# Tiles 4 to 7 transposed by VectorE, one spreading product for four tiles' scales, and VectorE for gate times up in the head

## The chip, the cores and the metric

The kernel runs on one core of a Trainium2 chip. The metric is device time in microseconds. The kernel before takes 787.4 us, the median of 3 runs (787.26 to 787.54). A core has TensorE (matrix products into PSUM), VectorE, ScalarE and GpSimd (element-wise work), SyncE (SP, which issues the DMAs here) and DMA engines. Each engine takes its own instructions strictly in the order in which the program lists them, and waits for others by semaphores.

## The reference

```python
def _A_ref(x, wqkv, wo):              # S = 2048, D = 640, 32 heads of 20
    qkv = (x @ wqkv) ...              # q, k, v
    idx = pos[:, None] - arange(8) * 2      # 8 earlier positions, two apart
    logits = einsum(q, kg) * scale          # kg, vg: k and v at idx
    attn = softmax(where(idx >= 0, logits, -1e9))
    return (attn weighted sum of vg) @ wo

def _B_ref(x, w_gate, w_up, w_down):  # F = 1536
    return ((x @ w_gate) * (x @ w_up)) @ w_down

xn = layernorm(x)
out = x + _A_ref(xn, wqkv, wo) * silu(_B_ref(xn, w_gate, w_up, w_down))
```

## The kernel before

**Tiles.** The 2048 rows are 16 tiles of 128. Tiles 0 to 7 hold the even positions, 8 to 15 the odd ones, as attention looks at positions two apart. The normalised rows are wanted transposed, as operands of TensorE: `xT` has four chunks of four tiles, each in a high and a low part (`hi`, `lo`). Every product is three products of such parts (`mm3`, L90 to L95: hi by hi, hi by lo, lo by hi).

**Two ways to transpose.** Tiles 0 to 7 go through `trans` (L218): VectorE scales the tile (`norm`, `apply`), TensorE transposes it in five pieces into PSUM, ScalarE copies out the high part and VectorE subtracts to get the low part. Tiles 8 to 15 go through `trans_odd` (L245): the tile is loaded a second time in another layout (`load_xq`, from `xq`), in which 32 x 32 blocks lie so that VectorE's own transpose (L249) makes the tile that is wanted. In that layout a partition holds pieces of four different rows, so mean and scale have to be spread to other partitions: `spread` (L236) does it by four products with the selection matrix `sel` for all eight tiles. The tile then takes four scalings of 160 columns, a transpose, a copy of the high part on ScalarE, and a subtraction for the low part, which `halves` holds back until the next tile has been transposed (`low_parts`).

**Units and pieces.** The heads are in six groups (5, 5, 5, 5, 6, 6); a unit is one group for the even or the odd positions, 12 in all. `qkv(u, i)` (L281) is q, k and v of unit u for tile i: 15 matmuls into one of four PSUM buffers "q", which ScalarE empties by two copies, into `kv` (L289) and `q` (L290). There are two `kv` buffers, one for even and one for odd units, so unit 2 writes where unit 0's attention reads. `attention(u)` (L298) is VectorE's, but for the exponentials on ScalarE (L333): four products and sums for the logits (L321, L324), the softmax, then four weighted products (L342) with sums between (L350) and the output (L353). `gate_up(f, ch)` (L379) is a piece: 15 matmuls for g, 15 for u, of 128 columns of F and 512 rows, each into one of two PSUM buffers. ScalarE copies g to `gs` (L389); the product of gate and up comes in `finish`: on VectorE (L400) while an attention is running, else by a copy of u on ScalarE (L402) and a product on GpSimd (L403). The result goes to DRAM. `finish` is called in the middle of the next piece, or at once where no attention is running.

**Order.** The order is written by hand: an engine's order is the order of the calls. Attention is a generator. `advance(budget)` adds to a credit, and lays down attention's next steps as long as the credit is above zero; each step takes its cost from it (1.85 for one of the large steps with 5 heads, 1.5 for a group of three small ones). A piece gives 3.25 in its middle and 3.25 at its end, a `qkv` 1.9. `begin_unit(u)` follows a `drain(u - 2)`, which lays down all that is left of that unit's attention.

**The head** (L656 to L702) normalises tiles 4 to 7 together, lays their TensorE transposes between pieces (0, 0) and (1, 0), then goes on with pieces (0, 1) and (1, 1) and the odd tiles. The first attention starts in unit 1 at i = 3; pieces (0, 2), (1, 2), (0, 3), (1, 3) follow, and from L733 on the units and pieces alternate.

Of the kernel before, what the change touches and what calls it, by code (L numbers as in the profile page):

```python
# [50 lines left out]
def kernel(  # L51
# [23 lines left out]
    def st(shape, tag, bufs, dt=F32):  # L75
        cnt[0] += 1
        return sb.tile(shape, dt, tag=tag, bufs=bufs, name=f"{tag}_{cnt[0]}")

    def pt(shape, tag, bufs):
        cnt[0] += 1  # L80
        return ps.tile(shape, F32, tag=tag, bufs=bufs, name=f"{tag}_{cnt[0]}")
# [37 lines left out]
    def load_wf(f):  # L119
        wf_raw[f] = st([P, KD, 2, P], "wraw", 3)  # L120
        nc.sync.dma_start(wf_raw[f], wgu[f])
# [58 lines left out]
    def moments(s0, n, mv=None):  # L180
        stats = st([P, n, 2, 6], "stats", 2)
        mv = st([P, n, 2], "mv", 2) if mv is None else mv
        for i in range(n):
            for a in range(2):
                nc.vector.bn_stats(stats[:, i, a, :], xt[s0 + i][:, a * HALF:(a + 1) * HALF])
            nc.vector.bn_aggr(mv[:, i, :], stats[:, i])
        return mv

    def rstd(var, out, n):
        r = st([P, 4, NE], "rstd", 2)[:, :, :n]  # L190
        nc.scalar.activation(r[:, 0, :], var, AF.Sqrt, bias=eps_t)
        step = 1 if n <= 2 else n
        for i in range(0, n, step):
            nc.vector.tensor_scalar_add(r[:, 1, i:i + step], var[:, i:i + step], EPS)
        nc.vector.reciprocal(r[:, 2, :], r[:, 0, :])
        if step == 1:
            for i in range(n):
                ve, a, b = (r[:, k, i:i + 1] for k in (1, 2, 3))
                nc.vector.tensor_scalar(b, a, a, ve, op0=ALU.mult, op1=ALU.mult)
                nc.vector.tensor_scalar(b, b, -0.5, 1.5, op0=ALU.mult, op1=ALU.add)  # L200
                nc.vector.tensor_scalar(out[:, i:i + 1], b, a, None, op0=ALU.mult)
            return
        nc.vector.tensor_mul(r[:, 3, :], r[:, 2, :], r[:, 2, :])
        nc.vector.tensor_mul(r[:, 3, :], r[:, 3, :], r[:, 1, :])
        nc.vector.tensor_scalar(r[:, 3, :], r[:, 3, :], -0.5, 1.5, op0=ALU.mult, op1=ALU.add)
        nc.vector.tensor_mul(out, r[:, 3, :], r[:, 2, :])

    def apply(y, m, r):
        nc.vector.tensor_scalar(y, y, m, r, op0=ALU.subtract, op1=ALU.mult)

    def norm(s0, n, mv=None):
        mv = moments(s0, n) if mv is None else mv
        r = st([P, n], "r", 2)
        rstd(mv[:, :, 1], r, n)
        for i in range(n):
            apply(xt[s0 + i], mv[:, i, 0:1], r[:, i:i + 1])

    def trans(s):  # L218
        hi, lo = xT_tile(s)
        for k0, k1 in ((0, 4), (4, KD)):  # L220
            p = pt([P, k1 - k0, P], "q", 4)
            for k in range(k0, k1):
                nc.tensor.transpose(p[:, k - k0, :], xt[s][:, k * P:(k + 1) * P], ident)  # L223
            nc.scalar.activation(hi[:, k0:k1, :], p, AF.Copy)  # L224
            nc.vector.tensor_sub(lo[:, k0:k1, :], p, hi[:, k0:k1, :].bitcast(F32))  # L225

    mvo = st([P, NE, 2], "mvo", 1)
    mro = st([P, 2, NE], "mro", 1)  # L230
    mrq = st([P, NQ, 2, NE], "mrq", 1)

    def load_xq(s, n, t):
        nc.sync.dma_start(t, xq[:, s - NE:s - NE + n, :])

    def spread():  # L236

        p = pt([P, NQ, 2, NE], "q", 4)
        for a in range(NQ):
            nc.tensor.matmul(p[:, a], sel[:, a], mro, start=True, stop=True)  # L240
        nc.scalar.activation(mrq, p, AF.Copy)

    halves = []

    def trans_odd(s):  # L245
        for a in range(NQ):
            apply(xt[s][:, a * QC:(a + 1) * QC], mrq[:, a, 0, s - NE:s - NE + 1], mrq[:, a, 1, s - NE:s - NE + 1])
        y = st([P, KD, P], "ot", 2)
        nc.vector.transpose(y.rearrange("p k (q i) -> p k q i", i=QB),  # L249
                            xt[s].rearrange("p (q k j) -> p k q j", q=NQ, j=QB))  # L250
        hi, lo = xT_tile(s)
        nc.scalar.activation(hi, y, AF.Copy)
        low_parts()
        halves.append(lambda: nc.vector.tensor_sub(lo, y, hi.bitcast(F32)))

    def low_parts():
        while halves:
            halves.pop(0)()
# [22 lines left out]
    def qkv(u, i, parts=ALL3):  # L281
        g, r = UN[u]
        c = GROUPS[g] * DH
        p = pt([P, 3 * c], "q", 4)
        hi, lo = xT[(r * NE + i) // TPC]
        t0 = (i % TPC) * P
        a, b = (hi[:, :, t0:t0 + P], lo[:, :, t0:t0 + P]), wq[g]
        mm3(p, [([t[:, k, :] for t in a], [t[:, k, :] for t in b]) for k in range(KD)], parts)
        nc.scalar.activation(kv_t[u][:, :, W - 1 + i, :], p[:, c:].rearrange("p (a c) -> p a c", a=2), AF.Copy)  # L289
        nc.scalar.activation(q_t[u][:, i, :], p[:, :c], AF.Copy)  # L290
        for i0, i1 in ((1, 5), (5, NE)):
            if i == i1 - 1:
                for p0, p1 in ((0, 112), (112, 127)):
                    nc.sync.dma_start(kv_t[u][p0 + 1:p1 + 1, :, i0 - 1:i1 - 1, :],
                                      kv_t[u][p0:p1, :, W - 1 + i0:W - 1 + i1, :])
# [80 lines left out]
    def gate_up_half(f, ch, n, p, c=slice(0, CH), **parts):  # L376
        mm3(p[:, c], [([t[:, k, n, :] for t in wf[f]], [t[:, k, c] for t in xT[ch]]) for k in range(KD)], **parts)

    def gate_up(f, ch, between=(), amid=(), part=None):  # L379
        if part is None:  # L380
            pp = [pt([P, CH], "g", 2), pt([P, CH], "u", 2)]
            c = slice(0, CH)
        else:
            pp, c = part, slice(CH // 2, CH)
        gate_up_half(f, ch, 0, pp[0], c)
        for act in amid:
            act()
        gs = st([P, CH], "gs", 2)
        nc.scalar.activation(gs, pp[0], AF.Copy)  # L389
        for act in between:  # L390
            act()
        share = (c.stop - c.start) / CH
        finish_piece()
        advance(PACE * 3.25 * share)
        gate_up_half(f, ch, 1, pp[1], c)

        def finish():
            hs = st([P, CH], "hs", 2)
            if running:
                nc.vector.tensor_mul(hs, pp[1], gs)  # L400
            else:
                nc.scalar.activation(hs, pp[1], AF.Copy)  # L402
                nc.gpsimd.tensor_mul(hs, hs, gs)  # L403
            nc.sync.dma_start(h_scr[ch * TPC:(ch + 1) * TPC, :, f, :].rearrange("t p c -> p t c"),
                              hs.rearrange("p (t c) -> p t c", c=P))

        unfinished.append(finish)
        if not running:
            finish_piece()
        advance(PACE * 3.25 * share)  # L410

# [2 lines left out]
    def finish_piece():  # L414

        while unfinished:
            unfinished.pop(0)()
# [232 lines left out]
    nc.gpsimd.memset(mask, 0.0)  # L650
    for i in range(NE - 1):
        nc.gpsimd.memset(mask[:, i, :W - 1 - i], MASKED)
    sel = st([P, NQ, P], "sel", 1)
    nc.gpsimd.tensor_copy(sel.rearrange("p q (b i) -> p q b i", i=QB),
                          ident.rearrange("p (q i) -> p q i", i=QB).unsqueeze(2).to_broadcast([P, NQ, NQ, QB]))
    norm(4, 4)  # L656
    qkv(0, 2)
    qkv(0, 3)
    gate_up(0, 0, part=part0)
    trans(4)  # L660
    trans(5)
    moments(8, 2, mvo[:, 0:2])
    gate_up(1, 0, amid=(lambda: trans(6),))
    moments(10, 2, mvo[:, 2:4])
    load_xq(8, 4, xc[:, 4:8])
    trans(7)
    load_wf(2)
    qkv(0, 4)
    qkv(0, 5)
    moments(12, 2, mvo[:, 4:6])  # L670
    moments(14, 2, mvo[:, 6:8])
    load_xq(12, 3, xa)
    load_xq(15, 1, xd)
    nc.vector.tensor_copy(mro[:, 0, :], mvo[:, :, 0])
    rstd(mvo[:, :, 1], mro[:, 1, :], NE)
    gate_up(0, 1, amid=(spread,))
    trans_odd(8)
    trans_odd(9)
    qkv(0, 6)
    trans_odd(10)  # L680
    qkv(0, 7)
    trans_odd(11)
    gate_up(1, 1, amid=(lambda: trans_odd(12),))
    trans_odd(13)
    begin_unit(1)
    for i in range(8):
        if i == 3:
            running.append((0, attention(0)))
        if i == 2:
            load_wq(1, ((0, 3), (3, 5)))  # L690
            low_parts()
        if i < 2:
            trans_odd(14 + i)
        qkv(1, i)
        advance(PACE * 1.9)
    running.append((1, attention(1)))
    split_wq(1, nc.gpsimd)
    gate_up(0, 2)
    gate_up(1, 2)
    gate_up(0, 3)  # L700
    split_wf(2, nc.gpsimd)
# [156 lines left out]
```

## Time and profile before

| | |
|---|---|
| median of 3 runs | 787.4 us |
| the profiled execution | 787.72 us |
| its span, first to last instruction | 785.8 us |
| TensorE busy | 778.8 us |
| VectorE busy | 659.0 us |
| ScalarE busy | 234.7 us |
| GpSimd busy | 147.3 us |
| granted TensorE clock | 1.00 |
| unit 1 on TensorE | from 60.13 us |
| first attention on VectorE | from 69.67 us |
| unit 2 on TensorE | from 104.61 us |
| last attention's output | at 533.46 us |
| output projection on TensorE | from 563.03 us |

In lines of the trace the first two numbers are the start in us from the span's start and the duration of the merged instructions; then come the engine (PE is TensorE, DVE VectorE, ACT ScalarE, POOL GpSimd), the line of the kernel, the operation, what it writes and reads, the shape and the number of instructions, and in brackets the idle time before it and what ended that. Busy times of TensorE overlap at their ends, so its pace is read from start to start. In lists of waits the numbers are us in total, how often, and the longest.

### The profile page before, as it was taken

The page shows a single profiled execution, that of the slowest core. Times are in us where ns is not written, and L with a number is a line of the kernel's source. Part 1 is how long each engine was busy: PE and PEld are TensorE (multiplying, and loading weights), DVE is VectorE, ACT ScalarE, POOL GpSimd, SP SyncE. Part 2 cuts the span into 40 slices and gives each one's busy share as a digit, 9 for nine tenths or more (in the row PEclk, how much of TensorE's full clock was granted, in tenths as well). Part 3 has the DMA queues.
Part 4 walks back from the last instruction along what each step waited for, and adds up shares of the span by engine and source line. Part 5 has one row for each costly group of instructions (what it writes and reads, how often), then busy time and mean ns, then how long its engine had stood idle before and what let it go on. Part 6 is the DMA issues. An engine that isn't in the chain of part 4 may idle for free.

```text
span 785.8 us, 11227 instructions
## 1 busy us (share of the span) xinstructions
PE 778.8 (99%) x4456; PEld 709.7 (90%) x4456; DVE 659.0 (84%) x660; ACT 234.7 (30%) x536; POOL 147.3 (19%) x110
## 2 busy tenths in 40 slices
PE   8999999999999999999999999999999999999997
PEld 6989898889898898899898989888899999999997
DVE  6889899999999979997999999992177667787775
ACT  5334211121112111311221202012366564444442
POOL 5201211022013200410231000112468600000000
PEclk9999999999999999999999999999999999999999
DMA  8272122141132322404033132332797574555534
GB/s 308 80 230 76 41 63 69 48 123 48 50 85 87 96 71 61 118 27 112 28 105 86 58 86 58 102 107 66 164 269 212 165 274 138 195 205 189 181 101 135
DMA packets 81661, 92.68 MB, mean 118 GB/s; under 512 B 23032, under 2 KB 63304, under 8 KB 81480
## 3 DMA queue, kind: packets, MB, share of 16 engines
q1 hardware_dynamic: 81608, 91.96, 38.2%
q8 instruction: 35, 0.57, 0.3%
q14 instruction: 18, 0.15, 0.1%
HBM read 54.53 MB, written 28.31 MB: 105 GB/s over the span
## 4 chain that ended last, share of the span: by engine, by line
PE 99%; DVE 0%; ACT 0%; issue 0%; POOL 0%; POOLq 0%
PE q L95 36%; PE u L95 21%; PE g L95 21%; PE q L598 11%; PE u L598 5%; PE g L598 3%; PE q L157 1%; PE q L223 1%; ACT xc L224 0%; PE q L240 0%; DVE xc L225 0%; DVE q L584 0%; DVE q L585 0%; ACT q L579 0%; POOL ident masks.py:199 0%
## 5 line engine op out<-in xcount | busy, mean ns | idle before, releaser
L95 PE MATMUL u<-xc,wf 128*128 128x512 f32 (+1 forms) x735 | 176.2, 391 | 0.0
L95 PE MATMUL g<-xc,wf 128*128 128x512 f32 (+1 forms) x735 | 176.1, 390 | 0.0
L95 PEld LDWEIGHTS u<-xc,wf 128*128 128x128 f32 x735 | 135.8, 188 | 32.1
L95 PEld LDWEIGHTS g<-xc,wf 128*128 128x128 f32 x735 | 135.4, 188 | 30.9
L95 PE MATMUL q<-wqh,xc 128*128 128x300 f32 (+1 forms) x960 | 159.7, 309 | 1.4 <-DVE xc L225 0.8
L95 PEld LDWEIGHTS q<-wqh,xc 128*128 128x128 f32 x960 | 146.0, 188 | 3.9 <-ACT xc L224 1.4
L321 DVE TENSOR_TENSOR t<-q,kv 128x1600 f32<-128x1600 f32 (+1 forms) x48 | 97.7, 2036 | 10.0 <-DMA kv<-kv 10.0
L342 DVE TENSOR_TENSOR t<-e,kv 128x1600 f32<-128x1600 f32 (+1 forms) x48 | 97.5, 2051 | 1.1
L86 POOL TENSOR_TENSOR wf<-wraw,wf 128x256 fp32r<-128x256 f32 (+2 forms) x22 | 48.5, 2223 | 248.0 <-ACT wf L85 229.8
L324 DVE TENSOR_REDUCE lg<-t 128x80 f32<-128x1600 f32 (+1 forms) x48 | 92.6, 1930 | 1.2
L389 ACT ACTIVATE gs<-g 128x512 f32<-128x512 f32 x48 | 28.7, 598 | 205.9 <-PE g L95 190.8
L95 PE MATMUL q<-wql,xc 128*128 128x300 f32 (+1 forms) x480 | 86.0, 309 | 0.0
L350 DVE TENSOR_TENSOR t<-t,t 128x1600 f32<-128x1600 f32 (+1 forms) x36 | 80.3, 2231 | 1.1
L95 PEld LDWEIGHTS q<-wql,xc 128*128 128x128 f32 x480 | 74.3, 188 | 0.0
L289 ACT ACTIVATE kv<-q 128x200 f32<-128x200 f32 (+1 forms) x96 | 33.4, 348 | 133.0 <-PE q L95 133.0
L598 PE MATMUL q<-xc,wf 128*128 128x320 f32 x432 | 67.3, 309 | 0.0
L598 PEld LDWEIGHTS q<-xc,wf 128*128 128x128 f32 x432 | 64.3, 188 | 0.0
L86 POOL TENSOR_TENSOR wql<-wraw,wqh 128x300 fp32r<-128x300 f32 (+4 forms) x15 | 33.2, 2238 | 142.8 <-ACT wqh L85 137.6
L95 PE MATMUL q<-wf,wf 128*128 128x320 f32 x156 | 35.7, 310 | 0.0
L400 DVE TENSOR_TENSOR hs<-u,gs 128x512 f32<-128x512 f32 x39 | 26.7, 683 | 0.7 <-issue 0.7
L95 PEld LDWEIGHTS q<-wf,wf 128*128 128x128 f32 x156 | 26.1, 189 | 0.0
L86 DVE TENSOR_TENSOR wf<-ot,wf 128x640 fp32r<-128x640 f32 x13 | 14.8, 1137 | 12.8 <-ACT wf L85 12.8
(161 smaller groups left out, 892.2 us busy)
## 6 DMA issues: line engine op xcount, KB each, us to landing
h_scr<-hs SPq DMA_DIRECT2D x48, 256.0 KB, 2.3
wraw<-in_wgu SPq DMA_DIRECT2D x12, 640.0 KB, 5.1
t<-h_scr SPq DMA_DIRECT2D x8, 768.0 KB, 7.2
hs<-s_scr SPq DMA_DIRECT2D x16, 320.0 KB, 4.3
gs<-in_x SPq DMA_DIRECT2D x16, 320.0 KB, 4.7
wraw<-h_scr SPq DMA_DIRECT2D x12, 384.0 KB, 6.0
out<-q SPq DMA_DIRECT2D x14, 320.0 KB, 3.4
wraw<-in_wd SPq DMA_DIRECT2D x12, 320.0 KB, 4.9
```

The costliest lines, as they stand in the source:

```text
L86: eng.tensor_sub(lo, raw, hi.bitcast(F32))
L95: nc.tensor.matmul(acc, a, b, start=first and n == 0, stop=last and n == len(runs) - 1)
L157: nc.tensor.matmul(pt([P, 3, P], "q", 4), ident, ident.unsqueeze(1).to_broadcast([P, 3, P]), start=True, stop=True)
L223: nc.tensor.transpose(p[:, k - k0, :], xt[s][:, k * P:(k + 1) * P], ident)
L289: nc.scalar.activation(kv_t[u][:, :, W - 1 + i, :], p[:, c:].rearrange("p (a c) -> p a c", a=2), AF.Copy)
L321: nc.vector.tensor_mul(t, q.rearrange("p i c -> p (i c)").unsqueeze(1).to_broadcast([P, 2, NE * c]), places(0, j))
L324: nc.vector.tensor_reduce(out=lg[:, :, j:j + 2].rearrange("p n a -> p a n"), in_=heads(t), op=ALU.add, axis=AX.X)
L342: nc.vector.tensor_mul(heads(t), pw, heads(places(1, j)))
L350: nc.vector.tensor_add(acc, acc, t)
L389: nc.scalar.activation(gs, pp[0], AF.Copy)
L400: nc.vector.tensor_mul(hs, pp[1], gs)
L598: nc.tensor.matmul(p, y[:, i, k], wd_t[name][k][:, l], start=new and r == 0, stop=r == len(runs) - 1, skip_group_check=True)
```

## The change

- Tiles 4 to 7 are transposed as the odd tiles are: loaded a second time from `xq`, which now holds tiles 4 to 15, scaled in four parts and transposed by VectorE. `trans_odd` becomes `trans_q`. The twenty TensorE transposes of these tiles go.
- Scales are spread for four tiles at a time, three times in all. `quarter` and a new `sel` replace the four selection matrices: VectorE multiplies the scales by a mask (`own`), and one product with `sel` of 32 columns spreads them.
- In the pieces of the head, and where no attention is running near the end, VectorE multiplies gate by up; only the very last piece keeps ScalarE and GpSimd. Pieces are then finished where `finish_piece` stands in the order, or in the next piece.
- The order of the head is another: pieces, statistics and reloads lie differently, `gate_up(0, 2)` stands between `qkv(1, 3)` and `qkv(1, 4)`, and the first attention starts after it with a credit of -4.

```diff
+    def scales(s0):
+        mv, mr = stat[s0]
+        nc.vector.tensor_copy(mr[:, 0, :], mv[:, :, 0])
+        rstd(mv[:, :, 1], mr[:, 1, :], TPC)
+        own[s0] = st([P, NQ, 2, TPC], "own", 2)
+        nc.vector.tensor_mul(own[s0], mr.unsqueeze(1).to_broadcast([P, NQ, 2, TPC]),
+                             quarter.unsqueeze(2).unsqueeze(3).to_broadcast([P, NQ, 2, TPC]))
+
+    def spread(s0):
+
+        p = pt([P, NQ, 2, TPC], "q", 4)
+        nc.tensor.matmul(p, sel, own[s0], start=True, stop=True)
+        spread_t[s0] = st([P, NQ, 2, TPC], "mrq", 2)
+        nc.scalar.activation(spread_t[s0], p, AF.Copy)
...
-        for a in range(NQ):
-            nc.tensor.matmul(p[:, a], sel[:, a], mro, start=True, stop=True)
-        nc.scalar.activation(mrq, p, AF.Copy)
...
-            if running:
+            if not last:
                 nc.vector.tensor_mul(hs, pp[1], gs)
             else:
                 nc.scalar.activation(hs, pp[1], AF.Copy)
                 nc.gpsimd.tensor_mul(hs, hs, gs)
...
-        if not running:
+        if last:
             finish_piece()
...
-    norm(4, 4)
+    for i in range(TPC):
+        moments_q(4 + i, 1)
+        load_xq(4 + i, 1, xc[:, i:i + 1])
+    scales(4)
+    moments_q(8, 2)
     qkv(0, 2)
     qkv(0, 3)
     gate_up(0, 0, part=part0)
-    trans(4)
-    trans(5)
-    moments(8, 2, mvo[:, 0:2])
-    gate_up(1, 0, amid=(lambda: trans(6),))
-    moments(10, 2, mvo[:, 2:4])
-    load_xq(8, 4, xc[:, 4:8])
-    trans(7)
+    spread(4)
+    trans_q(4)
+    finish_piece()
+    trans_q(5)
+    gate_up(1, 0)
     load_wf(2)
+    trans_q(6)
+    trans_q(7)
     qkv(0, 4)
     qkv(0, 5)
-    moments(12, 2, mvo[:, 4:6])
-    moments(14, 2, mvo[:, 6:8])
+    low_parts()
+    finish_piece()
+    moments_q(10, 2)
+    load_xq(8, 4, xc[:, 4:8])
+    scales(8)
+    qkv(0, 6)
+    qkv(0, 7)
+    moments_q(12, 4)
     load_xq(12, 3, xa)
     load_xq(15, 1, xd)
-    nc.vector.tensor_copy(mro[:, 0, :], mvo[:, :, 0])
-    rstd(mvo[:, :, 1], mro[:, 1, :], NE)
-    gate_up(0, 1, amid=(spread,))
-    trans_odd(8)
-    trans_odd(9)
-    qkv(0, 6)
-    trans_odd(10)
-    qkv(0, 7)
-    trans_odd(11)
-    gate_up(1, 1, amid=(lambda: trans_odd(12),))
-    trans_odd(13)
+    scales(12)
+    gate_up(0, 1, amid=(lambda: spread(8),))
+    trans_q(8)
+    trans_q(9)
+    finish_piece()
+    trans_q(10)
+    gate_up(1, 1, amid=(lambda: spread(12),))
+    trans_q(11)
     begin_unit(1)
-    for i in range(8):
-        if i == 3:
-            running.append((0, attention(0)))
-        if i == 2:
+    trans_q(12)
+    finish_piece()
+    for i in range(TPC):
+        if i == 1:
             load_wq(1, ((0, 3), (3, 5)))
-            low_parts()
-        if i < 2:
-            trans_odd(14 + i)
+        qkv(1, i)
+    trans_q(13)
+    trans_q(14)
+    gate_up(0, 2)
+    trans_q(15)
+    low_parts()
+    credit[0] = -4.0
+    running.append((0, attention(0)))
+    for i in range(TPC, NE):
         qkv(1, i)
         advance(PACE * 1.9)
     running.append((1, attention(1)))
     split_wq(1, nc.gpsimd)
-    gate_up(0, 2)
     gate_up(1, 2)
     gate_up(0, 3)
```

More of the change, by code (lines that the diff above doesn't have):

```diff
@@ L225, in trans, with moments_q, trans_q @@
             nc.vector.tensor_sub(lo[:, k0:k1, :], p, hi[:, k0:k1, :].bitcast(F32))
-    mvo = st([P, NE, 2], "mvo", 1)
-    mro = st([P, 2, NE], "mro", 1)
-    mrq = st([P, NQ, 2, NE], "mrq", 1)
-    def load_xq(s, n, t):
-        nc.sync.dma_start(t, xq[:, s - NE:s - NE + n, :])
-    def spread():
-        p = pt([P, NQ, 2, NE], "q", 4)
-        for a in range(NQ):
-            nc.tensor.matmul(p[:, a], sel[:, a], mro, start=True, stop=True)
-        nc.scalar.activation(mrq, p, AF.Copy)
-    halves = []
-    def trans_odd(s):
-        for a in range(NQ):
-            apply(xt[s][:, a * QC:(a + 1) * QC], mrq[:, a, 0, s - NE:s - NE + 1], mrq[:, a, 1, s - NE:s - NE + 1])
+    stat = {s: (st([P, TPC, 2], "mvo", 3), st([P, 2, TPC], "mro", 3)) for s in range(TPC, NT, TPC)}
+    own, spread_t = {}, {}
+    def moments_q(s, n):
+        s0 = s // TPC * TPC
+        moments(s, n, stat[s0][0][:, s - s0:s - s0 + n])
+    def load_xq(s, n, t):
+        nc.sync.dma_start(t, xq[:, s - TPC:s - TPC + n, :])
+    def scales(s0):
[10 more added lines that the diff above has]
+        nc.scalar.activation(spread_t[s0], p, AF.Copy)
+    halves = []
+    def trans_q(s):
+        m, i = spread_t[s // TPC * TPC], s % TPC
+        for a in range(NQ):
+            apply(xt[s][:, a * QC:(a + 1) * QC], m[:, a, 0, i:i + 1], m[:, a, 1, i:i + 1])
         y = st([P, KD, P], "ot", 2)
@@ L384, in gate_up @@
             pp, c = part, slice(CH // 2, CH)
+        last = (f, ch) == (KF - 1, NCH - 1)
         gate_up_half(f, ch, 0, pp[0], c)
@@ L652 @@
         nc.gpsimd.memset(mask[:, i, :W - 1 - i], MASKED)
-    sel = st([P, NQ, P], "sel", 1)
-    nc.gpsimd.tensor_copy(sel.rearrange("p q (b i) -> p q b i", i=QB),
-                          ident.rearrange("p (q i) -> p q i", i=QB).unsqueeze(2).to_broadcast([P, NQ, NQ, QB]))
-    norm(4, 4)
+    quarter, sel = st([P, NQ], "quarter", 1), st([P, P], "sel", 1)
+    nc.gpsimd.memset(quarter, 0.0)
+    for a in range(NQ):
+        nc.gpsimd.memset(quarter[a * QB:(a + 1) * QB, a:a + 1], 1.0)
+    nc.gpsimd.tensor_add(sel[:, :QB], ident[:, :QB], ident[:, QB:2 * QB])
+    for a in range(2, NQ):
+        nc.gpsimd.tensor_add(sel[:, :QB], sel[:, :QB], ident[:, a * QB:(a + 1) * QB])
+    nc.gpsimd.tensor_copy(sel[:, QB:].rearrange("p (b i) -> p b i", i=QB),
+                          sel[:, :QB].unsqueeze(1).to_broadcast([P, NQ - 1, QB]))
+    for i in range(TPC):
[3 more added lines that the diff above has]
+    moments_q(8, 2)
     qkv(0, 2)
@@ L836 @@
     arrays["xb"] = lay(arrays["x"].reshape(S, NQ, KD, QB).transpose(0, 2, 1, 3).reshape(S, D))
-    odd = arrays["x"].reshape(NQ, QB, NE, DIL, NQ, QC)[:, :, :, 1]
-    arrays["xq"] = lay(odd.transpose(3, 1, 2, 0, 4).reshape(P, NE, D))
+    quarters = arrays["x"].reshape(NQ, QB, NE, DIL, NQ, QC).transpose(3, 4, 1, 2, 0, 5).reshape(DIL, P, NE, D)
+    arrays["xq"] = lay(np.concatenate([quarters[0][:, TPC:], quarters[1]], axis=1))
     q3 = np.asarray(A_wqkv).reshape(D, 3, D)
```

## The prediction

> **What bounds the kernel now.** I read the page first: shares, slices, chain. Then the list of what TensorE waits for, then the order of time of TensorE, ScalarE and VectorE around the instructions that the change touches, and last the distance between each piece's product on VectorE and the matmul that needs its PSUM buffer back.
>
> ```profile
> PE 778.8 (99%) x4456; PEld 709.7 (90%) x4456; DVE 659.0 (84%) x660; ACT 234.7 (30%) x536; POOL 147.3 (19%) x110
> PE 99%; DVE 0%; ACT 0%; issue 0%; POOL 0%; POOLq 0%
> ```
> ```profile
> PE q L157 <- POOL ident masks.py:199: 1.4, 1, 1.4
> PE q L95 <- DVE xc L225: 0.8, 1, 0.8
> PE q L95 <- ACT xc L224: 0.6, 1, 0.6
> ```
>
> The end is set by TensorE alone. It waits three times in 785.8 us, 2.8 us in all, never after 20.07 us. So every TensorE instruction removed is worth its full length, and every new wait costs its full length; VectorE counts only through the waits that it makes.
>
> **What TensorE loses and gains.** The 20 transposes of tiles 4 to 7 and the four spreading products go.
>
> ```profile
> 27.81 1.25 PE L223 MATMUL q<-ident,xc 128*128 128x128 f32 x10
> 28.82 3.75 PE L95 MATMUL g<-xc,wf 128*128 128x512 f32 x15
> 32.41 0.71 PE L223 MATMUL q<-ident,xc 128*128 128x128 f32 x5
> 32.87 3.74 PE L95 MATMUL u<-xc,wf 128*128 128x512 f32 x15
> 36.44 0.71 PE L223 MATMUL q<-ident,xc 128*128 128x128 f32 x5
> 36.91 0.94 PE L95 MATMUL q<-wqh,xc 128*128 128x300 f32 x5
> ...
> 44.62 0.96 PE L240 MATMUL q<-mro,sel 128*128 128x16 f32 x8
> 45.43 3.74 PE L95 MATMUL u<-xc,wf 128*128 128x512 f32 x15
> ```
>
> Counted from start to the next start (busy times overlap): 1.01 + 0.46 + 0.47 = 1.94 us of transposes and 0.81 us of spreading. In place of the four spreading products there are three (for tiles from 4, 8 and 12), each of 32 columns. The trace counts two instructions to a product: eight took 0.81 us, 0.10 each, so the six new ones take 0.61 us; as matmuls of 300 columns (2.06 us for 15, 0.14 each) they would be 0.82. I take 0.61, from the row of the operation that they replace. TensorE's saving is 2.75 - 0.61 = **2.14 us**, between 1.93 and 2.75.
>
> **Is the head in time?** VectorE's part of a tile goes from one scaling and two subtractions to four scalings (1.2 us), a transpose (0.77) and a subtraction (0.70), the 2.67 us at which the odd tiles follow each other (51.84, 54.52, 57.21); each head piece adds a product of 0.61. I walk VectorE from 20.92, where tiles 4 to 7 have their statistics now. Scales of tile 4 are ready at 26.7, statistics of 8 and 9 at 28.8; the spreading product follows TensorE's piece at 27.8 and ScalarE's copy of it (0.22) ends by 28.6. Tile 4 is transposed at 30.8, then the piece's product, tile 5 at 33.4, tile 6 at 36.1, tile 7 at 38.7; high halves 0.8 later, low halves at 34.1, 36.8, 39.4 and 40.3. TensorE wants tile 4 at 35.2, 5 at 37.3, 6 at 39.3 and 7 at 41.4, the low halves 1.4 later each: nothing waits. The four extra reloads (320 KB each) are issued from 22 to 25.5 on SP, which holds nothing else until 30.00, with the DMA engines 30% busy from 20 to 30; loads of this size took 2.3 to 4.7 us, and the first is wanted at 28.8. The reload of tiles 8 to 11 moves from 39.1 to about 42.9, behind the statistics of 10 and 11; with the 6.7 us to landing that it had, it is there at 49.6, and VectorE, through with statistics and scales of 12 to 15, asks at 50.5. The walk goes on in steps of 2.67: tile 8 at 52.5, tile 11's low half at 63.8 (wanted at 65.4), tile 15's at 73.2. No wait, and the first attention begins on VectorE at 73.2 instead of 69.67. Cover is thinnest at the 0.9 us of that reload.
>
> GpSimd's new memsets and sums end near 24, three microseconds ahead of their use, and its 1.3 us products (L403) with ScalarE's copies of u go. In the tail four more pieces move to VectorE, which sits idle there for 21.07 us: nothing.
>
> **Where the new wait comes from.** Attention's instructions are laid among the matmuls by credit. Its exponentials come when 17.3 is spent (1.0, eight steps of 1.85, a group of 1.5). Before, five advances of 1.9 and three of 3.25 make 19.25 in the middle of gate_up(1, 2). Now the count is set to -4 and gate_up(0, 2) pays nothing: -4 + 4 x 1.9 + 4 x 3.25 is 16.6 at the end of gate_up(0, 3), so the exponentials fall to the middle of gate_up(1, 3), 14 us of matmuls later. VectorE comes there early: five steps and a product after 73.2 it is at 82.8, and the product of piece (1, 2) next in its order needs u, which ends at 90.6 - 2.1 = 88.5. On ScalarE the exponentials stand behind the copy of g of gate_up(1, 3).
>
> ```profile
> 83.61 3.66 PE L95 MATMUL g<-xc,wf 128*128 128x512 f32 x15
> 87.37 0.60 ACT L389 ACTIVATE gs<-g 128x512 f32<-128x512 f32 x1 [6.40 <-PE g L95]
> 87.99 1.28 ACT L333 ACT_TABLE_LOAD   x1
> 89.28 0.47 ACT L333 ACTIVATE e<-lg 128x320 f32<-128x320 f32 x1
> 89.79 0.49 DVE L335 TENSOR_REDUCE sm<-e 128x40 f32<-128x320 f32 x1 [3.33 <-ACT e L333]
> 91.28 3.56 DVE L342 TENSOR_TENSOR t<-e,kv 128x1600 f32<-128x1600 f32 x2
> 106.88 0.34 ACT L289 ACTIVATE kv<-q 128x200 f32<-128x200 f32 x1 [4.92 <-PE q L95]
> ```
>
> The reader sees the chain: g ends (87.27), copy, table load, exponentials, and VectorE goes on 2.52 us after g. The same chain from g of gate_up(1, 3), now ending at 101.27, less 2.1, at 99.1: VectorE goes on at 101.7 (its logits are ready by 99 even with GpSimd's split in the way), starts the weighted products 1.49 later, and the last that reads k and v is the sixth of 1.83 us: 114.1. Unit 2 writes the same buffer. TensorE begins it at 104.61 - 2.1 = 102.5 and can fill four PSUM buffers, 4 x 2.06: until 110.7. Then the first must have been emptied, and ScalarE's copy of it into kv (0.34, waiting for PSUM only at 106.88) is held until 114.1, and with the second copy (0.48 for both) until 114.6. **TensorE waits 3.9 us**, whatever the head saves, since both ends hang on TensorE's own time. Above: a product caught behind a GpSimd split took 4.48 instead of 1.82, so up to 6.6. Below: nothing, were the copy not held.
>
> **What is late next.** The first attention now ends, with its last sum, output and a product of 0.61, at 117.5. The second took 36.0 us with that product; it ends 8.0 us later than its 144.69, TensorE is 1.8 later, so VectorE lags 6.2. The credit is 4.0 short too, which puts each piece's product about two attention steps earlier in VectorE's order. Piece (3, 0): 6.2 - 3.7 for two steps, against a slack of 2.8 us. Piece (3, 3): 6.2 - 2.7, against 4.1. Piece (4, 2) has the least:
>
> ```profile
> 256.62 0.68 DVE L400 TENSOR_TENSOR hs<-u,gs 128x512 f32<-128x512 f32 x1
> 258.27 3.66 PE L95 MATMUL u<-xc,wf 128*128 128x512 f32 x15
> ```
>
> The matmul at 258.27 uses this product's buffer: slack 0.97, and 6.2 - 2.65 (a step of 1.74, an output of 0.91) - 0.97 leaves 2.6 us of waiting. At 293.48 VectorE waited 4.34 us for a transfer, so the lag doesn't outlive unit 5. Between 0 (the lag eaten up on the way) and 2.6 I take 1.8, nearer to the row that shows the shortage.
>
> **Sum.** On the profiled span of 785.8 us (787.72 with what lies around it; the median is 787.4): -2.1 + 3.9 + 1.8 = +3.6. On the median, **791.0 us**.
>
> **A stalled TensorE may come back slow.**
>
> ```profile
> 1.37 5.49 PE L157 MATMUL q<-ident 128*128 128x384 f32 x8 [1.37 <-POOL ident masks.py:199]
> 7.55 0.81 PE L157 MATMUL q<-ident 128*128 128x384 f32 x2
> ```
>
> After the start, eight matmuls took 0.69 each; later the same took 0.40, though the granted clock reads 1.00 throughout. A cold array costs 8 x 0.28 = 2.3 us. The waits of 0.6 and 0.8 us left no such trace; one of 3.9 is not in it. The Trainium skill, "TensorE: Matmul & The Clock Gate", section "Why this matters for your kernels", says to leave no TensorE gap over about 3 us, as one idle window halves the clock. By that rule 2.3 us are added here, by the short waits none. It is a rival.
>
> **Rivals and chances.**
> - Forecast, both waits: 791.0, own range 789 to 793, 43%.
> - Only the wait at unit 2, VectorE's slack takes the rest: 787.4 - 2.1 + 3.9 = 789.2, 17%. For it: no such wait in the trace of before; against: 0.97 us of slack.
> - The other side: the copy is not held, as the weighted products end 4 us sooner than I think. Only the removed matmuls count: 785.3, 15%. It decides at 110.2: is the last read of kv done by then? For it speaks that kv was free at 105.40 before, 1.5 ahead of the copy; against, that the exponentials can't leave the place the credit gives them.
> - The head is late: the reload of tiles 8 to 11 lands as slowly as that of tiles 12 to 14 (9.7 instead of 6.7), 2.1 us past VectorE's 50.5. Tile 11's slack of 1.6 turns to 0.5 of waiting, the lag grows 2.1: 791.0 + 2.6 = 793.6, 13%.
> - The cold array after the wait: 793.3, 12%.
>
> Faster by over 0.2% (1.6 us, about what can be told from no change) is the third: 0.15. Unit 2 alone lies at the bound of 789.0; with half of it, 0.09 is no change; slower 0.76. The range 786.5 to 795 leaves out most of the third case and twice-late heads.
>
> **What would show it.** Right: a wait of TensorE of about 4 us before the fifth qkv of unit 2, released by ScalarE's copy, with the kv copy waiting for VectorE; the exponentials behind the fourth copy of g after the head; VectorE idle 5 us before the product of piece (1, 2) and 4 to 5 before L335; 20 transposes left at L223. Wrong: no TensorE wait past 100 us, or a wait in the head, or matmuls of unit 2 after the wait slower than 2.06 us for 15.

## The result and the profile after

The changed kernel takes 792.73 us (median of 6 runs, 792.52 to 793.25) against 787.7 us before in the same runs: a ratio of 1.0064, with a 95% interval of 1.0054 to 1.0075. The profiled execution spans 790.7 us, 4.9 more than before.

The page's busy times and its chain that ended last:

```profile
PE 779.0 (99%) x4434; PEld 710.1 (90%) x4434; DVE 668.6 (85%) x691; ACT 230.8 (29%) x527; POOL 130.0 (16%) x110
PE 86%; DVE 10%; issue 2%; DMA 1%; ACT 1%; SPq 0%; DVEq 0%
```

Busy shares hardly differ from before; the chain does. It was TensorE from end to end, and now leaves TensorE for VectorE over a tenth of the span. The list of TensorE's waits (us in total, times, longest) says through which door:

```profile
PE q L95 <- ACT q L302: 3.8, 1, 3.8
PE q L157 <- POOL ident masks.py:199: 1.4, 1, 1.4
PE q L95 <- DVE xc L225: 0.8, 1, 0.8
PE q L95 <- ACT xc L224: 0.6, 1, 0.6
PE u L95 <- DVE hs L413: 0.4, 1, 0.4
PE q L223 <- issue: 0.3, 1, 0.3
```

The three old waits of the head are there unchanged, and 0.3 us that nothing in the profile explains lie near the start, at 6.56. Two new waits stand past 100 us. The first, in TensorE's order of time:

```profile
28.10 0.31 PE L250 MATMUL q<-own,sel 128*128 128x32 f32 x2
28.24 3.74 PE L95 MATMUL g<-xc,wf 128*128 128x512 f32 x15
...
110.23 0.85 PE L95 MATMUL q<-wqh,xc 128*128 128x300 f32 x5
114.85 1.62 PE L95 MATMUL q<-wqh,xc 128*128 128x300 f32 x5 [3.77 <-ACT q L302]
116.26 1.45 PE L95 MATMUL q<-wql,xc 128*128 128x300 f32 x5
117.52 1.85 PE L95 MATMUL q<-wqh,xc 128*128 128x300 f32 x10
119.21 0.86 PE L95 MATMUL q<-wql,xc 128*128 128x300 f32 x5
```

Four qkv of unit 2 have run, the fifth has no PSUM buffer. Behind the wait the matmuls are slow: 20 of them take from 114.85 to 119.21, 4.36 us, where 20 at 0.138 are 2.76. That is 1.6 us more, and the granted clock reads 0.68 from 115 to 120 us. ScalarE's order of time shows what held the buffer:

```profile
99.32 0.60 ACT L402 ACTIVATE gs<-g 128x512 f32<-128x512 f32 x1 [3.34 <-PE g L95]
99.94 1.28 ACT L345 ACT_TABLE_LOAD   x1
101.23 0.47 ACT L345 ACTIVATE e<-lg 128x320 f32<-128x320 f32 x1
114.31 0.34 ACT L301 ACTIVATE kv<-q 128x200 f32<-128x200 f32 x1 [12.61 <-DVE t L354]
```

The exponentials stand behind the copy of g of gate_up(1, 3), and the copy into kv waits 12.61 us for VectorE. VectorE's side:

```profile
88.88 0.69 DVE L413 TENSOR_TENSOR hs<-u,gs 128x512 f32<-128x512 f32 x1 [6.17 <-issue]
...
101.74 0.49 DVE L347 TENSOR_REDUCE sm<-e 128x40 f32<-128x320 f32 x1 [4.69 <-ACT e L345]
...
112.40 1.82 DVE L354 TENSOR_TENSOR t<-e,kv 128x1600 f32<-128x1600 f32 x1
```

An engine that is about to be late idles 6.17 us before the product of piece (1, 2) and 4.69 us for the exponentials. Its last read of kv ends at 114.2.

Where TensorE starts the same piece in both kernels gives the account of the span:

| place on TensorE | before | after | difference |
|---|---|---|---|
| qkv(0, 2) | 20.07 | 20.30 | +0.2 |
| unit 2 | 104.61 | 102.63 | -2.0 |
| piece (2, 0) | 121.10 | 124.74 | +3.6 |
| u of piece (3, 2) | 183.07 | 187.42 | +4.4 |
| output projection | 563.03 | 567.70 | +4.7 |
| end of the span | 785.8 | 790.7 | +4.9 |

The head saves 2.2 us (from +0.2 to -2.0), unit 2 loses 5.6, and from there to u of piece (3, 2) another 0.7 go, 0.45 of them in the second wait.

### The profile page after: what moved, and what is told of

Its sections match the earlier page's. It is cut to its first block, busy times and chain, and to the rows that moved or that the text cites. A ratio compares the mean times of both kernels' runs of the same rounds, so it can differ in the third digit from the quotient of the medians.

```text
span 790.7 us, 11213 instructions
## 1 busy us (share of the span) xinstructions
PE 779.0 (99%) x4434; PEld 710.1 (90%) x4434; DVE 668.6 (85%) x691; ACT 230.8 (29%) x527; POOL 130.0 (16%) x110
## 4 chain that ended last, share of the span: by engine, by line
PE 86%; DVE 10%; issue 2%; DMA 1%; ACT 1%; SPq 0%; DVEq 0%
PE q L95 31%; PE u L95 18%; PE g L95 18%; PE q L611 11%; PE u L611 5%; PE g L611 3%; DVE t L354 3%; DVE t L362 2%; DVE t L333 2%; DVE lg L336 2%; DMA t<-in_xb 1%; DVE hs L413 1%; SPq L106 0%; DVE stats L185 0%; DVE e L349 0%
## 5 line engine op out<-in xcount | busy, mean ns | idle before, releaser
L95 PEld LDWEIGHTS q<-wqh,xc 128*128 128x128 f32 x960 | 147.8, 190 | 8.2 <-ACT q L302 4.0
L333 DVE TENSOR_TENSOR t<-q,kv 128x1600 f32<-128x1600 f32 (+1 forms) x48 | 100.0, 2083 | 7.2 <-DMA kv<-kv 7.2
L354 DVE TENSOR_TENSOR t<-e,kv 128x1600 f32<-128x1600 f32 (+1 forms) x48 | 99.9, 2098 | 1.1
L86 POOL TENSOR_TENSOR wf<-wraw,wf 128x256 fp32r<-128x256 f32 (+2 forms) x22 | 41.5, 1903 | 272.3 <-ACT wf L85 272.3
L362 DVE TENSOR_TENSOR t<-t,t 128x1600 f32<-128x1600 f32 (+1 forms) x36 | 75.3, 2091 | 1.1
L413 DVE TENSOR_TENSOR hs<-u,gs 128x512 f32<-128x512 f32 x47 | 32.1, 684 | 20.3 <-PE u L95 13.3
```

Source lines behind the costliest of these rows:

```text
L86: eng.tensor_sub(lo, raw, hi.bitcast(F32))
L95: nc.tensor.matmul(acc, a, b, start=first and n == 0, stop=last and n == len(runs) - 1)
L333: nc.vector.tensor_mul(t, q.rearrange("p i c -> p (i c)").unsqueeze(1).to_broadcast([P, 2, NE * c]), places(0, j))
L354: nc.vector.tensor_mul(heads(t), pw, heads(places(1, j)))
L362: nc.vector.tensor_add(acc, acc, t)
```

## The experiments

Each run is set against the kernel before on the same chip; ratios are of their times, with the 95% interval. Where no other base is named, the edit is to the changed kernel.

### Credit as if gate_up(0, 2) had paid

```diff
-    credit[0] = -4.0
+    credit[0] = 6.5
```

> The credit at the start of the first attention is 6.5 instead of -4, as if gate_up(0, 2) had paid. Pacing theory: the exponentials come behind the copy of g of gate_up(1, 2), two pieces earlier, the weighted products end near 107, before TensorE needs the fifth PSUM buffer at 110.9, and the wait of 3.8 us, the slow matmuls behind it (1.6 us) and the wait of 0.5 us in unit 3 all go: about 785.7 us, 2 under the kernel before. Rival, the added work on VectorE (669 us busy instead of 659) is what delays unit 2, wherever attention stands in the order: TensorE still waits 3 us or more there, 791 to 793 us.

787.1 us, ratio 0.9994 (0.9984 to 1.0003): no change that can be told from the kernel before, and 5.6 us under the changed one. The exponentials in ScalarE's order of time:

```profile
85.33 0.60 ACT L402 ACTIVATE gs<-g 128x512 f32<-128x512 f32 x1 [1.63 <-PE g L95]
85.95 1.28 ACT L345 ACT_TABLE_LOAD   x1
90.93 0.47 ACT L345 ACTIVATE e<-lg 128x320 f32<-128x320 f32 x1 [3.69 <-DVE lg L343]
```

They stand two pieces earlier and wait for VectorE now. The wait at unit 2 is gone, piece (2, 0) starts at 119.17, 1.9 us earlier than before. The pacing theory holds for this wait, and the rival that VectorE's load alone delays unit 2 falls. But the expected 785.7 was not reached, as the list of waits shows:

```profile
PE u L95 <- DVE hs L413: 0.9, 1, 0.9
```

This wait, of u of piece (3, 2) for the product of piece (3, 0), was to go as well and grew from 0.45 to 0.89. Its product stands one attention step later in VectorE's order than in the changed kernel: behind the last weighted product, where it was ahead of it.

### One unit of credit more

```diff
-    credit[0] = -4.0
+    credit[0] = -3.0
```

> The credit is -3 instead of -4. Pacing theory: 17.6 is paid at the end of gate_up(0, 3), just over the 17.3 that the exponentials need, so they move half a piece ahead and no longer stand behind the copy of g of gate_up(1, 3); VectorE goes on at about 97 instead of 101.7. GpSimd's split then lies beside the first weighted products and may hold one of them up to 2.7 us: the wait at unit 2 is 0 to 2 us, under the length that cools the array: 786 to 789 us. Rival, VectorE's load: a credit of 1 less changes nothing, 792.7.

791.9 us, ratio 1.0050 (1.0035 to 1.0065). The waits that differ:

```profile
PE u L95 <- DVE hs L413: 3.1, 1, 3.1
...
PE q L95 <- ACT q L302: 0.3, 1, 0.3
```

The exponentials moved as expected (they start at 94.90 instead of 101.23) and the wait at unit 2 fell from 3.8 to 0.3 us. Yet 3.1 us turn up at u of piece (3, 2). I had the first wait right and the second wrong. TensorE is ready for that matmul 4.3 us sooner than in the changed kernel, VectorE's attention runs 3.5 us sooner, but the product of piece (3, 0) comes only 1.7 us sooner (184.99 instead of 186.69): the one credit more puts it, too, behind the last weighted product. So of the 2.6 us by which this wait grew, 1.8 are the order and 0.8 that TensorE gained more than VectorE.

### The table loaded early

```diff
+    nc.scalar.activation(st([P, 1], "warm", 1), eps_t, AF.Exp)
     credit[0] = -4.0
```

> One exponential of a single column is put ahead of the first attention, so that the table load of 1.28 us falls where ScalarE is idle and leaves the chain from g to the exponentials. Chain theory: the wait at unit 2 shrinks from 3.8 to about 2.5 us; if the array then stays warm, the 1.6 us of slow matmuls go too: 789.8 us, with a cold array 791.4. Rival, VectorE is late for other reasons and the exponentials are not what it waits for: 792.7.

790.95 us, ratio 1.0045 (1.0030 to 1.0059). TensorE's order of time, and a window behind the wait (busy us of PE, PEld, DVE, ACT, POOL, then the granted clock, DMA share, GB/s):

```profile
110.02 0.85 PE L95 MATMUL q<-wqh,xc 128*128 128x300 f32 x5
113.22 1.62 PE L95 MATMUL q<-wqh,xc 128*128 128x300 f32 x5 [2.35 <-ACT q L302]
114.63 1.45 PE L95 MATMUL q<-wql,xc 128*128 128x300 f32 x5
```
```profile
114.00:117.00 3.00, 3.00 (x16) 3.00 (x15) 2.96 (x4) 0.29 (x2) 0.00 (x0) 0.59 0.19 51
```

With 1.28 us taken out of the chain the wait is 1.4 us shorter: the chain from g through the exponentials to the last weighted product sets it. The array is cold behind this shorter wait too, at a granted clock of 0.59, and 791.4 was the forecast for that.

### The wait filled

```diff
+            if u == 2 and i == 4:
+                w = pt([P, 3, P], "g", 2)
+                for _ in range(9):
+                    nc.tensor.matmul(w, ident, ident.unsqueeze(1).to_broadcast([P, 3, P]), start=True, stop=True)
             qkv(u, i)
```

> Nine products of the identity into a free buffer of g are put between the fourth and the fifth qkv of unit 2, 3.6 us at the pace of warm matmuls; they compute nothing that is used. Cold-array theory: the wait stays (filled), but the matmuls behind it run at 0.14 us from the first: 1.6 us less, 791.1 us. Rival, the slow matmuls behind the wait are a refill that any wait brings: no change, 792.7.

792.48 us, ratio 1.0059 (1.0044 to 1.0074). The nine products took 5.5 us instead of 3.6, so the time says little: no slow matmuls behind them, but 1.5 us of overrun in their place. I had given a product 0.40 us, which near the start is the time of one of its two matmuls; in a row a product takes 0.61.

With six of them:

> As the filled wait, with six fillers instead of nine: the nine took 5.5 us instead of the 3.6 that I had given them, 0.61 each, and overran the wait by 1.6. Six take 3.7 us and end with the wait. Cold-array theory: matmuls behind it at full pace, 1.6 us less than the changed kernel: 791.1 us. Rival, a refill that any wait brings: 792.7.

793.69 us, ratio 1.0077 (1.0062 to 1.0092). In TensorE's order of time:

```profile
111.17 4.03 PE L758 MATMUL g<-ident 128*128 128x384 f32 x12
115.10 0.95 PE L95 MATMUL q<-wqh,xc 128*128 128x300 f32 x5
115.89 0.85 PE L95 MATMUL q<-wql,xc 128*128 128x300 f32 x5
116.58 1.54 PE L95 MATMUL q<-wqh,xc 128*128 128x300 f32 x10
```

and first in its list of waits:

```profile
PE u L95 <- DVE hs L413: 1.9, 1, 1.9
```

The 20 matmuls now take 2.86 us: an idle array, not a refill, made them slow. But no time is won, as the wait at u of piece (3, 2) grows from 0.45 to 1.90. Here VectorE's order is that of the changed kernel and the product of piece (3, 0) comes at 186.90, where it came at 186.69. So slow matmuls and this wait pay the same debt: TensorE has to be as late as VectorE's product, and what it doesn't lose at the one place it loses at the other.

### GpSimd multiplies in the head again

```diff
-            if not last:
+            if running and not last:
```

This with the credit of 6.5.

> Credit 6.5 as in the first experiment, and the products of the pieces outside a running attention (four in the head, four near the end) go back to ScalarE's copy and GpSimd. Theory, VectorE's lag is what is left after the pacing is mended: the head saves it 4 x 0.61 = 2.4 us less what GpSimd's instructions of 1.3 us hold up, attention starts 1 to 2 us earlier than 73.0, and the wait of 0.9 us in unit 3 goes: about 786.3 us. Rival, the products are of no account for TensorE: as the first experiment, 787.1.

787.54 us, ratio 0.9996 (0.9986 to 1.0005), as the first experiment. The wait of 0.9 us stays, and attention starts on VectorE at 73.37, not earlier. GpSimd's products, and VectorE's scalings at the same times:

```profile
55.17 1.29 POOL L416 TENSOR_TENSOR hs<-hs,gs 128x512 f32<-128x512 f32 x1 [13.02 <-issue]
...
64.19 1.28 POOL L416 TENSOR_TENSOR hs<-hs,gs 128x512 f32<-128x512 f32 x1 [6.43 <-issue]
```
```profile
54.40 2.16 DVE L209 TENSOR_SCALAR xc<-xc,mrq 128x160 f32<-128x160 f32 x4
58.07 1.17 DVE L209 TENSOR_SCALAR xc<-xc,mrq 128x160 f32<-128x160 f32 x4
...
63.42 2.15 DVE L209 TENSOR_SCALAR t<-t,mrq 128x160 f32<-128x160 f32 x4
```

Four scalings beside a GpSimd product take 2.16 instead of 1.17; two such cases and a subtraction of 1.45 instead of 0.78 make 2.6 us, which eats the 2.4 us that VectorE saves. The Trainium skill, "SBUF — State Buffer", section "SBUF: two separate sides", states that VectorE and GpSimd share a pair of ports under a lock, and that, where both need it, the loser waits for the whole instruction; these rows agree, with 1.0 us lost to instructions of 1.3. So in this order it is of no account which engine multiplies.

### Only the products moved, in the kernel before

```diff
-            if running:
+            if running or ch < 2:
```

> The kernel before, with only the products of the head's four pieces on VectorE (and of two pieces near the end), where they stood. Theory: VectorE then waits in its order for u of piece (1, 0), until 36.5, ahead of the statistics that it did at 34.5, and the scales of the odd tiles come some 2 us late: TensorE waits 1 to 2 us at the spreading products, 788.6 to 789.6 us, and VectorE lags into attention. Rival, VectorE has room for them in the head: 787.6 or less, as GpSimd holds up nothing.

790.87 us, ratio 1.0041 (1.0026 to 1.0056). That is over the 788.6 to 789.6 that was expected. In the list of TensorE's waits:

```profile
PE q L95 <- ACT q L290: 1.5, 2, 1.2
...
PE q L240 <- DVE mro L206: 1.0, 1, 1.0
```

The wait at the spreading products is there (1.0), and 1.5 us in unit 1 that I had not named: VectorE idles 4.87 us for u of piece (0, 1), ahead of the transposes of the odd tiles, and ScalarE's copies of the high halves and out of PSUM come late with them. At 76.62 before, piece (0, 2) starts at 79.80 here. Where a product stands in VectorE's order weighs more than what it lasts: in this order, finished at once at the end of its piece, it costs 3.2 us; in the changed order nothing.

### Credit early, and given back at unit 2

```diff
-    credit[0] = -4.0
+    credit[0] = 6.5
...
+        if u == 2:
+            credit[0] -= 4.0
```

> Credit 6.5 at the start of the first attention, and 4 taken off at the start of unit 2, so that VectorE does not idle in the first attention and each later piece's product stands about two attention steps earlier in its order. Theory: no wait at unit 2, none at (3, 2): 0.9 us under the first experiment, 786.2 us, and under the kernel before by 1.4. Rival, the lag only moves: a drain at a later unit makes TensorE wait again, 787 or more.

786.05 us, ratio 0.9981 (0.9972 to 0.9991). Once more, for the size:

> The version with 6.5 at the first attention and 4 taken off at unit 2 once more, for its size: 786.1 us, 0.2% under the kernel before, and no wait of TensorE past 21 us.

786.11 us, ratio 0.9979 (0.9970 to 0.9988), and TensorE's whole list of waits:

```profile
PE q L157 <- POOL ident masks.py:199: 1.4, 1, 1.4
PE q L95 <- DVE xc L225: 0.8, 1, 0.8
PE q L95 <- ACT xc L224: 0.6, 1, 0.6
PE q L95 <- POOL wql L86: 0.2, 1, 0.2
```

The waits of the kernel before, but for 0.2 us. This version beats both kernels, the one before by 0.2%: it is the saving of the head without the new waits. Against the first experiment only the order after unit 2 differs. VectorE sums the second softmax of the even positions at the same time in both (163.41 there, 163.47 here), but the product of piece (3, 0) comes at 175.40 instead of 181.56, and the wait of 0.9 us is gone.

### The same total, all of it taken at the start

```diff
-    credit[0] = -4.0
+    credit[0] = 2.5
```

> Credit 2.5 at the start of the first attention: the same total from unit 2 on as 6.5 with 4 taken off there, but 4 less in the first attention. Theory, both where the credit lies and how much there is count: the exponentials fall behind the copy of g of gate_up(0, 3), VectorE goes on at about 95.3 instead of 91.4, 4 us of it idle; no wait or a short one at unit 2, and about 1 to 3 us of waiting at (3, 2): 787 to 789 us. Rival, only the total credit counts: 786.1, as the run with 6.5 and 4 taken off.

791.54 us, ratio 1.0043 (1.0030 to 1.0057), over the 787 to 789 that was expected. VectorE's idle time for the exponentials, and TensorE's first wait in the list:

```profile
94.36 0.49 DVE L347 TENSOR_REDUCE sm<-e 128x40 f32<-128x320 f32 x1 [3.71 <-ACT e L345]
```
```profile
PE u L95 <- DVE hs L413: 3.3, 2, 3.1
```

VectorE idles as expected. But from unit 2 on the two runs don't have the same credit, though the expectation says so. `drain` lays down what is left of the first attention and takes nothing off the credit. By the kernel's own costs, with 6.5 that attention is paid in full by unit 2 (33.2 of the 33.6 given); with 2.5 its last sum and its output, 2.9 in all, are laid down free. So this run enters unit 2 some 2.9 ahead of the best version. VectorE's order around the product of piece (3, 0), here and in the best version's second run:

```profile
177.78 4.45 DVE L362 TENSOR_TENSOR t<-t,t 128x1600 f32<-128x1600 f32 x1
182.26 1.82 DVE L354 TENSOR_TENSOR t<-e,kv 128x1600 f32<-128x1600 f32 x1
184.01 0.68 DVE L413 TENSOR_TENSOR hs<-u,gs 128x512 f32<-128x512 f32 x1
```
```profile
173.66 1.83 DVE L354 TENSOR_TENSOR t<-e,kv 128x1600 f32<-128x1600 f32 x1
175.40 0.68 DVE L413 TENSOR_TENSOR hs<-u,gs 128x512 f32<-128x512 f32 x1
```

The product stands behind two more steps, the sum of 4.45 us and a weighted product of 1.82, and comes 8.6 us later; VectorE's lag itself makes 2.4 of that (its softmax sum starts at 165.88 instead of 163.47). The two steps are 6.3 us, more than the wait of 3.1, while the 2.4 alone would have fitted into the 4.7 us that lie between product and matmul in the best version. By these rows it is the order after unit 2 that brings this wait, and not the 3.71 us of idling; no run has that idling with the best version's order. Whether only the total of the credit counts stays untested, as the two totals differ.

## Why the prediction was right, point by point

- **TensorE bounds the kernel, and each wait counts in full.** Right: the 4.9 us of the span are found on TensorE, place by place.
- **The matmuls removed: -2.14 us.** Right: -2.2. The spreading product of 32 columns takes 0.14 us from start to start (28.10 to 28.24), not 0.20; three cost 0.42.
- **The head is in time.** Right, to a tenth or two: the first transposed tile at 30.8, the first attention at 73.12 (73.2 in the walk), no wait, 20 transposes left at L223. The reload of tiles 8 to 11 was no matter.
- **The wait at unit 2: 3.9 us.** Right in place, size (3.77) and cause, and VectorE's idle times that go with it are there (6.17 and 4.69). The copy is held for 12.61 us, so the rival that it isn't held falls. That the credit is the cause was argued from a count; the runs with 6.5, -3 and 2.5 show it by shifting the credit alone, and the early table load shows that the chain through the exponentials sets the length.
- **What is late next: 1.8 us.** The mechanism is right, its place and its share are not. The shortage came at the product of piece (3, 0), which I had put at 6.2 - 3.7 - 2.8, no wait by 0.3 us, and not at (4, 2). The two steps and the slack were as I had them. The lag was smaller, as the slow matmuls make TensorE late too: ahead of (3, 0) VectorE is 8.1 us later than before and TensorE 3.7, a lag of 4.4; ahead of (4, 2) it is 6.9 and 4.4, a lag of 2.5, and nothing waits there. What I had left out at (3, 0) is where GpSimd's splits of weights fall (here from 172.03 for 6.71 us and from 181.91 for 3.17), and what they hold up on VectorE:

```profile
171.89 5.51 DVE L354 TENSOR_TENSOR t<-e,kv 128x1600 f32<-128x1600 f32 x2
177.43 2.98 DVE L362 TENSOR_TENSOR t<-t,t 128x1600 f32<-128x1600 f32 x1
...
182.31 4.46 DVE L362 TENSOR_TENSOR t<-t,t 128x1600 f32<-128x1600 f32 x1
186.69 0.68 DVE L413 TENSOR_TENSOR hs<-u,gs 128x512 f32<-128x512 f32 x1
```

At 1.82 an instruction these take 5.7 us more than they need, all ahead of the product; before it was 3.0 us, as the second split's hold-up came behind it. 4.4 - 3.7 - 2.8 + 2.7 makes 0.6, and 0.45 was measured. With a warm array the wait is 1.9, near the 1.8 that I had given, but at another place: as a size that is luck.

- **The cold array.** A rival with 12%, and one of the signs of being wrong that I had named, and it came true: 1.6 us of slow matmuls against the 2.3 taken from the start of the kernel, at a granted clock of 0.68 from 115 to 120 us. Its price as a rival, added on top of the forecast, was wrong: the filled wait shows that these 1.6 us only replace the later wait. The rule of the Trainium skill, "TensorE: Matmul & The Clock Gate", section "Why this matters for your kernels", of gaps up to about 3 us agrees with the changed kernel (3.77 us, cold), not with the early table load, where 2.35 us were enough.
- **The sum.** 791.0 against 792.73. The -2.1 and the 3.9 stand as forecast. The 1.8 is made of two other things, 1.6 us of slow matmuls and 0.45 of waiting at another piece, so that this term agrees is in part luck. The rest is 0.3 us of slightly slower matmuls in units 2 and 3 (2.08 us instead of 2.06 for 15), 0.3 us on the way to the output projection and 0.2 us behind it, which I did not follow, and 0.2 us at the start, there before the change begins.
- **The products on VectorE: nothing.** Right for the changed order; the reason that I gave, room in the head and in the tail, is half of it. The other half is that GpSimd's product costs VectorE as much as it spares it.

## What to carry to other kernels

When TensorE sets the end and another engine runs along it at almost the same pace, a saving on TensorE is kept only if that engine's work is moved forward by as much: look at what the change does to the order of the second engine, not at its busy time. Two waits behind the same late engine can be one debt: warming the array only moved the loss to the second wait, and the test is whether the lateness itself went. Look at the second engine's order as well: two steps more or less ahead of the product that is waited for moved it by 6.2 us here, and work that is laid down without being counted, as `drain` does, undoes a count that was set earlier. A count that paces work (here one number, -4 or 6.5 with 4 given back) can be worth more than the edit that it comes with.

## What the hardware showed unexpectedly

The length of a gap doesn't settle whether TensorE comes back slow. After 2.35 us (the table loaded early) five matmuls took 1.41 us from start to start instead of 0.69, with the granted clock at 0.59. After 3.09 us, with a credit of -3, it read 1.00 and the next 15 matmuls took 3.61 us from start to start, no more than after the wait of 0.45 us in the changed kernel (3.60); so after 3.11 us with 2.5. But these are single executions. The profiled ones, 790.81 and 789.83 us at a mean granted clock of 1.000 and 0.999, were not like the rest of their kernels: the other three of each took 791.86 to 792.39 with -3 and 791.40 to 791.75 with 2.5, all at 0.998. One stretch like that of the changed kernel, 0.68 for 5 us, lowers the mean by 0.002, so by this estimate the array came back slow there; no trace shows it. If so, the moment has a part in it, as all executions of a kernel run the same order.

Twelve 384-column matmuls of plain floats in a row took 0.33 us each, while 512-column ones of the split operands take 0.23.
